# Sparse attention and an eight-expert MoE on one Trainium2 core: second search's first round moved into the opening gather, and several orders changed

## The chip, the cores and the metric

One core of one Trainium2 chip runs the whole kernel. The time is device microseconds of one execution. Engines: PE (TensorE, matrix products), DVE (VectorE), ACT (ScalarE), POOL (GpSimd), and SP, which here only issues DMAs. Each engine works through its own instructions in the order in which they stand in its queue and waits on semaphores for the others.

## The reference

Attention over 8 batches, 8 heads, 576 positions and head size 64, with masks of stride 32 (local for the first four heads, strided for the other four). Its 4608 x 512 output goes to a mixture of eight experts with a capacity of 576 tokens each. Tokens are given to experts greedily, by descending gate logit over all (token, expert) pairs:

```python
logits = x @ w_gate
order = np.argsort(-logits.flatten())
for idx in order:
    tok, e = idx // E, idx % E
    if assigned[tok] >= 0 or counts[e] >= cap:
        continue
    assigned[tok] = e
    counts[e] += 1
for e in range(E):
    h = np.maximum(x[assigned == e] @ w1[e], 0.0)
    out[assigned == e] = h @ w2[e]
```

## The kernel before

The attention runs until about 177 us. Then the gate logits L of all tokens are closed (close_last, logits, summit), and the experts are filled one after the other: a "phase" (`ph`, 0 to 7) is one expert in the order in which they fill up.

To find which expert fills next and at which logit, the kernel searches thresholds. A search has seven rounds (`search`, six for the first one, `search0`): DVE compares the best remaining logits with 17 candidate values (`cm`, L862 in the first round, L865 later), PE counts (nine matmuls of L884), DVE copies the counts (`cp`, L888), PE folds them (four matmuls, L892), and DVE reduces to the next base `pm` (L901, L904) and makes the next candidates (`cand`, L868; `pre`, L875). After the search come the expert's number, its weights' loads and scales, the slots of its tokens (`slots`), the list of tokens that are left (`close`), and the token numbers (`indices`: a prefix matmul at L956, a scan on DVE at L962, `rv` at L998, the "rows" matmuls at L1012 that turn it into rows, and `pick` at L1020).

Rows: POOL gathers five tiles of rows of x from memory (`xr`, L1129), ACT and DVE split them into an upper and a lower fp16 half (`xg`, L1118 and L1119), and SP issues DMA transposes into `xt` (L1120). For the first expert the transposes are done by PE (L1110), with ACT (L1111) and DVE (L1112) taking the halves out of PSUM.

Weights: SP loads w1 and w2 in four pieces of 512 KB each; ACT squares them (`jk`, L1051) for a scale (`ss`, L1057; matmul at L1059; L208 to L213), ACT makes the upper halves (`w1h`, `w2h`, L1069) and DVE the lower halves (`w1l`, `w2l`, L1070). The fp32 buffer of each weight is single, so a load waits until DVE has taken the lower half of the weight before.

Each phase's products, `hidden` (L1226) and the output stage (L1278), are three fp16 products for each fp32 one: w1h by the upper and the lower half of `xt`, w1l by the upper half. A hidden block has 12 such terms over two column halves; `hh` (ACT, L1233) and `hl` (DVE, L1234) take the result out of PSUM, which has three such buffers. Results `y` (L1288) are scattered by POOL (L1289).

While PE works on phase `ph`, the work for the next experts is threaded into it. PE's order is written by hand: a clock counts the nanoseconds of issued matmuls, each chain of side work has a due time (the numbers `yield`ed, the constants T_...), and the due chain is advanced (`advance`). ACT's order is by hand in phase 0 only; the others' queues are scheduled by priority at build time. In the opening (183 to 215 us) the order is by hand too: `first_round` lays the list of close operations, in which the second search's first compare, the scale's matmul and the first transposes are inserted; HEAT gives counts of dummy matmuls (L1151) in that stretch.

## Time and profile before

| | us |
|---|---|
| median of 3 runs | 667.06 (661.7 to 668.71) |
| the profiled execution | 658.78 |
| its span in the profile | 657.0 |
| PE busy | 583.7 (89%) |
| DVE busy | 461.2 (70%) |
| ACT busy | 328.6 (50%) |
| POOL busy | 108.8 (17%) |
| DMA | 103.4 MB, 157 GB/s mean |

Phases begin, by the first hidden product, at 215.0, 276.6, 334.5, 388.1, 442.0, 496.1, 546.9 and 604.6 us; the last ends at about 652. PE is the engine with most work; a wait of PE in this part of the program is time lost, where a wait of another engine costs nothing unless PE meets it. The granted clock (PEclk) tells at which share of full speed the array ran.

### The profile page before, as it was taken

What the parts mean: (1) busy time and instruction counts of PE and PEld (TensorE: products, weight loads), DVE (VectorE), ACT (ScalarE), POOL (GpSimd) and SP (SyncE); (2) the same over time, 40 slices, a digit from 0 to 9 for tenths busy, and PEclk for the clock granted to TensorE, in tenths of its full rate; (3) what the DMA queues carried; (4) which work ended last, traced back from release to release, by engine and by line L of the source; (5) the groups of instructions that cost most, each with busy time, mean ns of one, the idle gap of its engine ahead of it and who ended that gap; (6) DMA issues with size and microseconds to landing.
All of it is one profiled execution on the core that took longest, in us unless ns stands there. A gap on an engine that the chain in (4) does not pass through costs nothing.

```text
span 657.0 us, 19687 instructions
## 1 busy us (share of the span) xinstructions
PE 583.7 (89%) x8220; PEld 370.8 (56%) x8220; DVE 461.2 (70%) x1431; ACT 328.6 (50%) x553; POOL 108.8 (17%) x124
## 2 busy tenths in 40 slices
PE   7888787898847789899989999999989998799996
PEld 4566565666533665475457457547637645555752
DVE  5878787887887897878697786776787755572210
ACT  2555463654303574842953951862564477562211
POOL 2011100111102001400410420330160131302011
PEclk9779999998957899999999999999999999799999
DMA  8778798786506507804833931860780585741001
GB/s 255 213 250 238 229 274 239 238 245 206 150 2 211 142 1 266 208 1 156 247 72 116 256 103 34 287 137 17 273 169 33 186 239 178 207 82 50 7 25 48
DMA packets 78480, 103.40 MB, mean 157 GB/s; under 512 B 41624, under 2 KB 49522, under 8 KB 78391
## 3 DMA queue, kind: packets, MB, share of 16 engines
q1 hardware_dynamic: 70311, 80.59, 41.9%
q0 software_dynamic: 7360, 21.15, 10.5%
q8 instruction: 64, 1.05, 0.7%
q10 hardware_dynamic: 720, 0.39, 0.2%
q14 instruction: 25, 0.20, 0.1%
HBM read 74.58 MB, written 18.87 MB: 142 GB/s over the span
## 4 chain that ended last, share of the span: by engine, by line
PE 23%; issue 14%; DVE 13%; DMA 8%; ACT 5%; POOL 3%; POOLq 0%; SPq 0%; DVEq 0%; ACTq 0%
PE ph L1226 15%; DMA w<-in_w_dram 5%; PE ph L1278 5%; DVE w1l L1070 2%; POOL xr L1129 2%; ACT jk L1051 2%; DMA xr<-x_scr,idx 2%; DVE cm L865 2%; DVE w2l L1070 1%; POOL out_dram L1289 1%; DVE xg L1119 1%; ACT w2h L1069 1%; DVE hl L1234 1%; ACT w1h L1069 1%; ACT hh L1233 1%
## 5 line engine op out<-in xcount | busy, mean ns | idle before, releaser
L1226 PE MATMUL ph<-xt,w1h 128*128 128x288 f16 (+2 forms) x1024 | 176.0, 289 | 4.8 <-DMA xt<-xg 1.8
L1226 PEld LDWEIGHTS <-w1h 128*128 128x128 f16 x1024 | 98.6, 99 | 30.9 <-issue 3.4
L1226 PE MATMUL ph<-xt,w1l 128*128 128x288 f16 (+2 forms) x512 | 112.1, 289 | 0.0
L1051 ACT ACTIVATE jk<-w 128x1024 f16<-128x1024 f32 x64 | 67.3, 1052 | 66.6 <-DMA w<-in_w_dram 66.2
L1278 PE MATMUL ph<-w2h,hh 128*128 128x512 f16 x256 | 97.2, 380 | 0.0
L1278 PE MATMUL ph<-w2h,hl 128*128 128x512 f16 x256 | 97.1, 379 | 0.0
L1278 PE MATMUL ph<-w2l,hh 128*128 128x512 f16 x256 | 97.0, 379 | 0.0
L1233 ACT ACTIVATE hh<-ph 128x576 f16<-128x576 f32 (+2 forms) x72 | 42.7, 593 | 100.3 <-PE ph L1226 100.3
L1234 DVE SCALAR_TENSOR_TENSOR hl<-ph,hh 128x576 f16<-128x576 f32 (+2 forms) x72 | 49.4, 686 | 57.0 <-ACT hh L1233 56.7
L1289 POOL DMA_INDIRECT out_dram<-y,idx x40 | 47.6, 1190 | 222.0 <-ACT y L1288 204.2
L1278 PEld LDWEIGHTS <-hh 128*128 128x128 f16 x512 | 48.3, 98 | 54.7 <-issue 3.7
L1129 POOL DMA_INDIRECT xr<-x_scr,idx x40 | 41.4, 1035 | 160.4 <-DVE idx L1024 125.1
L1226 PEld LDWEIGHTS <-w1l 128*128 128x128 f16 x512 | 49.7, 98 | 14.3 <-issue 1.8
L1070 DVE SCALAR_TENSOR_TENSOR w1l<-w,w_sw,w1h 128x512 f16<-128x512 f32 x64 | 45.9, 742 | 10.1 <-ACT w1h L1069 10.1
L1070 DVE SCALAR_TENSOR_TENSOR w2l<-w,w_sw,w2h 128x512 f16<-128x512 f32 x64 | 45.5, 742 | 8.2 <-ACT w2h L1069 8.2
L1069 ACT ACTIVATE w2h<-w,w_sw 128x512 f16<-128x512 f32 x64 | 41.1, 709 | 10.3 <-DVE w_sw L213 10.2
L1069 ACT ACTIVATE w1h<-w,w_sw 128x512 f16<-128x512 f32 x64 | 42.3, 708 | 2.6 <-DVE w_sw L213 1.5
L1288 ACT ACTIVATE y<-ph,so 128x512 f32<-128x512 f32 x32 | 21.8, 680 | 42.4 <-PE ph L1278 41.1
L1278 PEld LDWEIGHTS <-hl 128*128 128x128 f16 x256 | 25.0, 98 | 29.4 <-issue 2.1
L468 POOL DMA_DIRECT2D x_scr<-xs x23 | 14.9, 655 | 151.8 <-DVE vsum L307 96.3
L393 ACT ACTIVATE pr<-spa 128x576 f32<-128x576 f32 x32 | 20.7, 648 | 29.5 <-PE spa L390 28.1
L1119 DVE TENSOR_TENSOR xg<-xr,xg 128x512 f16<-128x512 f32 (+1 forms) x37 | 25.0, 688 | 12.0 <-ACT xg L1118 11.9
(542 smaller groups left out, 878.5 us busy)
## 6 DMA issues: line engine op xcount, KB each, us to landing
w<-in_w_dram SPq DMA_DIRECT2D x64, 512.0 KB
v_s<-in_ns_dram SPq DMA_DIRECT2D x28, 195.0 KB
kl<-in_kl_dram SPq DMA_DIRECT2D x16, 304.0 KB
ks<-in_ks_dram SPq DMA_DIRECT2D x16, 288.0 KB
qs<-in_qt_dram SPq DMA_DIRECT2D x16, 288.0 KB
ql<-in_qt_dram SPq DMA_DIRECT2D x16, 288.0 KB
x_scr<-xl SPq DMA_DIRECT2D x8, 512.0 KB
v_l<-in_nl_dram SPq DMA_DIRECT2D x16, 162.5 KB
```

The costliest lines, as they stand in the source:

```text
L393: nc.scalar.activation(pr[:, :S].rearrange("k (h n) -> k h n", h=2), u.sp[p][:, :, :HS], AF.Exp, scale=0.125)
L1051: nc.scalar.activation(jk, wf[:, c * n4:(c + 1) * n4].rearrange("p c f -> p (c f)"), AF.Square, scale=1.41422, accum_out=sq[:, c:c + 1])
L1069: nc.scalar.activation(hi[:, c, f], wf[:, c, f], AF.Copy, scale=s_)
L1070: nc.vector.scalar_tensor_tensor(lo[:, c, f], wf[:, c, f], s_, hi[:, c, f], op0=OP.mult, op1=OP.subtract)
L1119: nc.vector.tensor_tensor(xs[:, 1], xv, xs[:, 0], op=OP.subtract)
L1129: nc.gpsimd.indirect_dma_start(out=xr[:n], out_offset=None, in_=x_rows, in_offset=bass.IndirectOffsetOnAxis(ap=idx[:n, t:t + 1], axis=0))
L1226: nc.tensor.matmul(tile_[:, j, :w], wt[:, d, f * 128:(f + 1) * 128], xt[:, d // 2, xx, d % 2, c], start=(k == 0), stop=(k == 3 * DC - 1))
L1233: nc.scalar.activation(hv, src, AF.Relu)
L1234: nc.vector.scalar_tensor_tensor(lv, src, 0.0, hv, op0=OP.max, op1=OP.subtract)
L1278: nc.tensor.matmul(py, a[:, f, ts_], w[:, f], start=(k == 0), stop=(k == len(todo) - 1))
L1288: nc.scalar.activation(y, py, AF.Copy, scale=so[:, t:t + 1])
L1289: st = nc.gpsimd.indirect_dma_start(out=out_rows, out_offset=bass.IndirectOffsetOnAxis(ap=idx[:n, t:t + 1], axis=0), in_=y[:n], in_offset= ...
```

## The change

- close_last: the logits of the batch before the last, and the point operations of their peaks, move ahead of the last turn of the attention.
- pre0: the first `pre` (128 x 18) is made before the index chain. In `search` the separate `cand` operation falls away, since `pre` is now one operation with two operands; it is made after the yield instead of before.
- first_round: the close list has no insertions any more. After it come the take, round 0 of the second search, and round 1's compare; the scale follows (`after()`) behind the count, the heat of 20 and 3 and 1 around it, then the transposes and the rest.
- split order: the first w1 splits (k = 0 and 1) of phase 0 are ordered behind the two operations that take the transposed tiles.
- hidden: the first two blocks of the first column block go term by term (four of w1h by upper, four of w1h by lower, four of w1l by upper) instead of row chunk by row chunk.
- X2: the second search's third round waits 900 instead of 100.
- T_HOT7, T_LAST: the eighth expert's number, weights and indices come later.
- rows_of: at a phase's end the waiting loop advances only the fetch of that phase, and does not move the clock.

Instructions: DVE 1386 to 1357; PE 6166 to 6167 matmuls; ACT, POOL and SP as many as before. The diff, cut:

```diff
-X1 = 100
+X1, X2 = 100, 900
-HEAT = (8, 18, 5)
+HEAT = (8, 20, 3)
+T_HOT6, T_CLOSE6, T_HOT7, T_LAST = 3200, 9000, 9000, 6000
...
+            logits(B - 2, ps_b.tile([128, 512], F32, name="spb"))
+            ahead_ = summit(2, edge, (B - 1) * S // TP)
+            ahead_[0]()
             p2 = ps_b.tile([128, 512], F32, name="spb")
...
-                    cand = rt.tile([128, J1 + 1], F32, name="cand18")
-                    nc.vector.tensor_scalar(cand, pre, pm, None, op0=OP.add)
...
-                n = 1 if rd == R1 - 2 else J1 + 1
-                if not last:
-                    pre = cand[:, 0:1]
-                    if n > 1:
-                        pre = rt.tile([128, n], F32, name="pre1")
-                        nc.vector.tensor_scalar(pre, steps[:, rd + 1, :n], cand[:, 0:1], None, op0=OP.add)
-            yield pace(T_COUNT) + (X1 if len(closed) == 1 else T_FIRST if rd == 0 else 0)
+            yield pace(T_COUNT) + ((X2 if rd == 2 else X1) if len(closed) == 1 else T_FIRST if rd == 0 else 0)
             with urgent():
+                if rd and not last:
+                    n = 1 if rd == R1 - 2 else J1 + 1
+                    base, pre = pre[:, 0:1], rt.tile([128, n], F32, name=f"pre{n}")
+                    nc.vector.tensor_scalar(pre, steps[:, rd + 1, :n], pm, base, op0=OP.add, op1=OP.add)
...
-        yield T_HOT1 if ph == 1 else T_HOT6 if ph == E - 2 else T_HOT
+        yield {1: T_HOT1, E - 2: T_HOT6, E - 1: T_HOT7}.get(ph, T_HOT)
...
+                if ph == 0 and nch == DC and k <= 1:
+                    if k == 1:
+                        behind(a, turned[0])
+                    behind(b, turned[1])
...
+        nc.vector.tensor_scalar(pre0, steps[:, 1, :J1 + 1], cand0[:, 0:1], None, op0=OP.add)
         idx, sx = drain(indices(0, slot))
...
-            todo.insert(SCALE_AT, after)
-            todo.insert(SCALE_AT + 1, lambda: heat(HEAT[2]))
-            todo.insert(TURN_AT, lambda: [f() for f in first[:TURN_E]])
-            todo.insert(TAKE_AT, lambda: parts_.append(take(slot, src[0])))
-            todo.insert(SEARCH_AT, lambda: parts_.append(next(gen)))
             for f in todo:
                 f()
-            parts_[0]()
+            rest_ = take(slot, src[0])
+            next(gen)
+            next(gen)
+            heat(1)
+            after()
+            step = next(gen)
+            heat(HEAT[2])
+            for f in first[:TURN_E]:
+                f()
+            rest_()
...
+            if ph == E - 1:
+                yield T_LAST
             with urgent():
                 ei, code = number(w8)
...
+        terms = [(wt, xx, d) for d in range(DC) for wt, xx in ((w1h, 0), (w1h, 1), (w1l, 0))]
+        if n == 1 and f < 2 and js[0].start == 0:
+            terms = [(wt, xx, d) for wt, xx in ((w1h, 0), (w1h, 1), (w1l, 0)) for d in range(DC)]
...
-                    c = min(chains, key=lambda c: c[0])
-                    clock = max(clock, c[0])
+                    c = rows_of.get(ph) or min(chains, key=lambda c: c[0])
+                    if ph not in rows_of:
+                        clock = max(clock, c[0])
                     advance(c)
```

Three places show what moves. First ACT at the turn from phase 5 to phase 6. `w1h` (of w_8710 or w_8705) and `w2h` (of w_8719 or w_8714) are the seventh expert's, the `jk` of w_9164 or w_9162 the eighth's w1. Before:

```order
L1069 ACTIVATE w1h<-w_8710,w_sw_8716 128x4x128
L1288 ACTIVATE y<-ph,so 128x512
L1051 ACTIVATE jk,sq<-w_9164 128x1024 x2
L1069 ACTIVATE w2h<-w_8719,w_sw_8725 128x512 x4
L1288 ACTIVATE y<-ph,so 128x512
L1069 ACTIVATE w2h<-w_8719,w_sw_8725 128x512 x4
L1051 ACTIVATE jk,sq<-w_9164 128x1024
L1233 ACTIVATE hh<-ph 128x576
```

and of the changed kernel:

```order
L1075 ACTIVATE w1h<-w_8705,w_sw_8711 128x4x128 x2
L1304 ACTIVATE y<-ph,so 128x512
L1075 ACTIVATE w2h<-w_8714,w_sw_8720 128x512 x5
L1251 ACTIVATE hh<-ph 128x576
L1075 ACTIVATE w2h<-w_8714,w_sw_8720 128x512 x3
L1057 ACTIVATE jk,sq<-w_9162 128x1024
L1251 ACTIVATE hh<-ph 128x576
L1057 ACTIVATE jk,sq<-w_9162 128x1024 x2
```

The squares of the eighth expert's w1 stood ahead of the seventh's w2 splits; they now stand behind all of them, between the `hh`.

Second, DVE in the opening. Before, from the end of the close list (L204) to the halves of the transposed tiles (L1112):

```order
L204 TENSOR_TENSOR ohn<-ohn,wmn 128x288
L1057 TENSOR_REDUCE ss<-sq 128x1
L208 TENSOR_SCALAR ss_e<-pr__4339 128x1
L209 TENSOR_SCALAR ss_e<-ss_e 128x1
L210 TENSOR_SCALAR ss_e<-ss_e 128x1
L213 TENSOR_SCALAR w_sw_4187<-ss_e 128x2
L982 TENSOR_SCALAR pen<-slot 128x36
L983 TENSOR_TENSOR rmn<-rmn,pen 128x36
L862 TENSOR_TENSOR cm<-rmn,cand_3841 128x612
L875 TENSOR_SCALAR pre_4356<-steps,cand_3841 128x18
L1070 SCALAR_TENSOR_TENSOR w1l<-w_4181,w_sw_4187,w1h 128x4x128 x2
L1112 TENSOR_TENSOR xt<-ph,xt 128x2x2x128 x2
```

and of the changed kernel, from the second search's first compare (L872) on:

```order
L872 TENSOR_TENSOR cm<-rmn,cand_3841 128x612
L894 CAST cp<-pr__4346 128x68
L1063 TENSOR_REDUCE ss<-sq 128x1
L208 TENSOR_SCALAR ss_e<-pr__4361 128x1
L209 TENSOR_SCALAR ss_e<-ss_e 128x1
L210 TENSOR_SCALAR ss_e<-ss_e 128x1
L213 TENSOR_SCALAR w_sw_4188<-ss_e 128x2
L907 SCALAR_TENSOR_TENSOR g_4372,ne<-pr__4346,steps 128x17
L910 TENSOR_REDUCE pm<-ne 128x1
L875 SCALAR_TENSOR_TENSOR cm<-pre_3842,pm,rmn 128x612
L885 TENSOR_SCALAR pre_4429<-steps,pm,pre_3842 128x18
L1122 TENSOR_TENSOR xt<-ph,xt 128x2x2x128 x2
```

The compare, with the `pen` and `rmn` before it, stands ahead of the scale's sum; the next compare follows behind the scale, and the halves of the transposed tiles stand ahead of the first lower weight halves.

Third, POOL, whose queue carries the gathers (`xr`) and the scatters (`out_dram`); the rows of the changed kernel with the gathers for phases 4, 5 and 6:

```order
L1139 DMA xr<-x_scr,idx 128x512 x2
L1305 DMA out_dram<-y,idx 4608x512
L1139 DMA xr<-x_scr,idx 128x512 x2
L1139 DMA xr<-x_scr,idx 64x512
L1305 DMA out_dram<-y,idx 4608x512 x5
L1139 DMA xr<-x_scr,idx 128x512 x4
L1139 DMA xr<-x_scr,idx 64x512
L1305 DMA out_dram<-y,idx 4608x512 x3
L1139 DMA xr<-x_scr,idx 128x512
L1305 DMA out_dram<-y,idx 4608x512
```

Before, the five gathers of a phase always stood together; here an output row stands between the second and the third gather, and later behind a first one.

## Rows read from the trace of the kernel before

**Rows 1.** The page's part 1: busy us (share) and instructions of each engine.

```profile
PE 583.7 (89%) x8220; PEld 370.8 (56%) x8220; DVE 461.2 (70%) x1431; ACT 328.6 (50%) x553; POOL 108.8 (17%) x124
```

**Rows 2.** Waits of PE, 215 to 652: tile, line, releaser: total, times, longest us.

```profile
PE pr__9288 L1012 <- DVE rv L998: 5.5, 1, 5.5
PE ph L1226 <- DMA xt<-xg: 1.8, 2, 1.2
PE pr__4810 L884 <- DVE cm L862: 1.8, 1, 1.8
PE pr__6086 L884 <- DVE cm L865: 1.4, 1, 1.4
...
PE pr__5872 L1059 <- DVE p L1015: 1.2, 1, 1.2
```

**Rows 3.** Stretches: length, busy PE, PEld, DVE, ACT, POOL, PEclk, DMA share, GB/s.

```profile
215.00:651.90 436.90, 413.09 (x3341) 253.70 (x3340) 292.80 (x878) 232.06 (x396) 83.14 (x74) 0.99 0.45 132
215.00:248.98 33.98, 29.13 (x289) 21.52 (x289) 30.31 (x99) 20.28 (x40) 0.00 (x0) 0.95 0.22 61
276.58:303.08 26.50, 25.31 (x244) 19.40 (x245) 18.84 (x58) 9.59 (x16) 0.97 (x1) 1.00 0.06 15
303.08:334.52 31.44, 27.27 (x216) 12.83 (x214) 24.71 (x82) 21.41 (x37) 10.64 (x10) 1.00 0.84 239
467.07:496.06 28.99, 27.05 (x214) 12.64 (x212) 21.75 (x64) 21.04 (x37) 12.45 (x9) 1.00 0.80 215
546.94:580.87 33.93, 27.62 (x234) 20.67 (x233) 19.68 (x44) 23.34 (x41) 6.06 (x6) 0.90 0.71 198
604.64:628.16 23.52, 23.52 (x194) 18.79 (x193) 5.30 (x7) 5.25 (x8) 0.97 (x1) 1.00 0.03 12
```

**Rows 4.** Order of time, PE, phase 6: start, us, line, operation, [idle before].

```profile
562.33 1.51 PE L1012 MATMUL pr__9288<-ohl,rv 128*32 128x64 f16 x36 [5.47 <-DVE rv L998]
...
563.99 1.17 PE L1226 MATMUL ph<-xt,w1h 128*128 128x288 f16 x4
...
568.35 0.65 PE L1226 MATMUL ph<-xt,w1h 128*128 128x288 f16 x4
```

**Rows 5.** Order of time, ACT, turn of phase 5 to 6.

```profile
548.22 1.06 ACT L1051 ACTIVATE jk<-w 128x1024 f16<-128x1024 f32 x1 [4.35 <-DMA w<-in_w_dram]
...
550.72 2.54 ACT L1069 ACTIVATE w2h<-w,w_sw 128x512 f16<-128x512 f32 x4
```

**Rows 6.** Order of time, DVE, phase 6.

```profile
557.14 0.29 DVE L962 TENSOR_TENSOR_SCAN inc<-ones_f,pr__9220 128x72 f32<-128x72 f32 x1
...
561.62 0.66 DVE L998 TENSOR_TENSOR rv<-ohh,val 128x972 f16<-128x972 f16 x1
```

**Rows 7.** Order of time, POOL's first gather, and PE, start of phase 1.

```profile
261.41 0.98 POOL L1129 DMA_INDIRECT xr<-x_scr,idx  x1 [0.30 <-DVE ss_e L208]
...
278.06 0.54 PE L1226 MATMUL ph<-xt,w1h 128*128 128x288 f16 x3 [1.19 <-DMA xt<-xg]
```

**Rows 8.** Order of time, gather of phase 4's rows: POOL, SP, PE.

```profile
419.88 0.98 POOL L1129 DMA_INDIRECT xr<-x_scr,idx  x1 [29.14 <-DVE idx L1024]
...
425.75 8.80 SPq L1120 DMA_TRANSPOSE xt<-xg  x5
...
441.99 0.65 PE L1226 MATMUL ph<-xt,w1h 128*128 128x288 f16 x4
```

**Rows 9.** Order of time, DVE, opening.

```profile
211.52 0.16 DVE L1057 TENSOR_REDUCE ss<-sq 128x1 bf16<-128x4 f32 x1 [1.77 <-ACT jk L1051]
...
212.98 0.80 DVE L862 TENSOR_TENSOR cm<-rmn,cand 128x612 f16<-128x612 f32 x1
...
215.16 1.28 DVE L1112 TENSOR_TENSOR xt<-ph,xt 128x512 f16<-128x512 f32 x2
```

**Rows 10.** Order of time, PE, end of the first hidden block of phase 0.

```profile
219.17 0.98 PE L1110 MATMUL ph<-ident,xr 128*128 128x128 f32 x4
```

**Rows 11.** One line's instructions: `cand`, durations min/median/max, first and last start.

```profile
L868 DVE TENSOR_SCALAR cand<-pre,pm x30: 221/230/233, 223.6 to 502.8; 128x18 f32<-128x18 f32 x30
```

More of the change, by code (lines that the diff above doesn't have):

```diff
@@ L551, in close_last @@
             nc.vector.tensor_copy(xt[:, 1, b], p2[:, :b.stop - b.start])
+            for f in ahead_[1:-1]:
+                f()
             pb = ps_b.tile([128, 512], F32, name="spb")
@@ L556, in close_last @@
             nc.vector.tensor_scalar(lt[:, b], pb[:, :b.stop - b.start], sc, None, op0=OP.mult)
-            logits(B - 2, ps_b.tile([128, 512], F32, name="spb"))
-            for f in summit(2, edge, (B - 1) * S // TP):
-                f()
+            ahead_[-1]()
             logits(B - 1, po_all[:, 1])
@@ L764, in band_stride_attention_then_capacity_moe @@
     cand0 = r1.tile([128, J1 + 1], F32, name="cand0")
+    pre0 = r1.tile([128, J1 + 1], F32, name="pre0")
     def tables():
@@ L778, in band_stride_attention_then_capacity_moe, with behind @@
     scat, closed, first, second = [], [], [], []
-    ready, emitted, rush = set(), set(), set()
+    ready, emitted, rush, rows_of = set(), set(), set(), {}
+    turned = {}
+    def behind(ins, other):
+        tc.add_manual_dep(ins.ins, other.ins.name, mybir.DependencyInfo(mybir.DependencyClass.NoSync,
+                                                                        mybir.DependencyReason.DATA), reason="order")
     def urgent(ph=1):
@@ L853, in search @@
     def search(rm, ohc, more):
-        cand, src, top, pm = cand0, rm, None, None
+        cand, pre, src, top, pm = cand0, pre0, rm, None, None
         ohv = ohc.rearrange("p c e -> p (c e)")
@@ L1065, in parts, with split @@
                 return [(slice(k, k + 1), slice(0, width)) for k in range(nch)]
-            def split(c, f, k, wf=wf, sc=sc, hi=hi, lo=lo):
+            def split(c, f, k, wf=wf, sc=sc, hi=hi, lo=lo, nch=nch):
                 s_ = sc.bitcast(F32)[:, 0:1]
-                nc.scalar.activation(hi[:, c, f], wf[:, c, f], AF.Copy, scale=s_)
-                nc.vector.scalar_tensor_tensor(lo[:, c, f], wf[:, c, f], s_, hi[:, c, f], op0=OP.mult,
-                                               op1=OP.subtract)
+                a = nc.scalar.activation(hi[:, c, f], wf[:, c, f], AF.Copy, scale=s_)
+                b = nc.vector.scalar_tensor_tensor(lo[:, c, f], wf[:, c, f], s_, hi[:, c, f], op0=OP.mult,
+                                                   op1=OP.subtract)
+                if ph == 0 and nch == DC and k <= 1:
+                    if k == 1:
+                        behind(a, turned[0])
+                    behind(b, turned[1])
             todo.append([(T_SQ, lambda c=c, g=square: g(c)) for c in range(4)])
@@ L1110, in turn @@
                 nc.tensor.transpose(pt[:, c // 2, c % 2, :n], xr[:n, c * 128:c * 128 + 128], ident[:n, :n])
[L1111 to L1112 removed]
+            turned[0] = nc.scalar.activation(xs[:, 0], pt[..., :n], AF.Copy)
+            turned[1] = nc.vector.tensor_tensor(xs[:, 1], pt[..., :n], xs[:, 0], op=OP.subtract)
     def halve(ph, xt, xr, t, n):
@@ L1195, in side @@
             slot = yield from slots(ph, *src, code, mv)
-            chains.append([due_now() + (T_F if 1 < ph < E - 2 else 0), fetch(ph, slot, wts)])
+            rows_of[ph] = [due_now() + (T_F if 1 < ph < E - 2 else 0), fetch(ph, slot, wts)]
+            chains.append(rows_of[ph])
             if ph == E - 2:
@@ L1221, in hidden @@
         n = len(js)
-        for d in range(DC):
-            for wt, xs in ((w1h, (0, 1)), (w1l, (0,))):
-                for xx in xs:
-                    for j, c in enumerate(js):
-                        nc.tensor.matmul(tile_[:, j, :w], wt[:, d, f * 128:(f + 1) * 128],
-                                         xt[:, d // 2, xx, d % 2, c], start=(k == 0), stop=(k == 3 * DC - 1))
-                        yield w * 123 // HC
-                    k += 1
+        terms = [(wt, xx, d) for d in range(DC) for wt, xx in ((w1h, 0), (w1h, 1), (w1l, 0))]
+        if n == 1 and f < 2 and js[0].start == 0:
+            terms = [(wt, xx, d) for wt, xx in ((w1h, 0), (w1h, 1), (w1l, 0)) for d in range(DC)]
+        for wt, xx, d in terms:
+            for j, c in enumerate(js):
+                nc.tensor.matmul(tile_[:, j, :w], wt[:, d, f * 128:(f + 1) * 128], xt[:, d // 2, xx, d % 2, c],
+                                 start=(k == 0), stop=(k == 3 * DC - 1))
+                yield w * 123 // HC
+            k += 1
         hv, lv = (a[:, f, js[0].start:js[-1].stop].rearrange("p (j n) -> p j n", j=n) for a in (hh, hl))
@@ L1238, in ffn @@
         if ph == E - 1:
-            dr = nc.gpsimd.drain()
-            tc.add_manual_dep(dr.ins, scat[-1].ins.name, mybir.DependencyInfo(mybir.DependencyClass.NoSync,
-                                                                             mybir.DependencyReason.DATA), reason="pause")
+            behind(nc.gpsimd.drain(), scat[-1])
         hh = xp.tile([128, FC, CAP], F16, name="hh", bufs=1)
```

9 lines of the change are left out of this document (3 added, 6 removed).

## The prediction

> **What bounds the kernel now.** I read the page first: PE works 89% of the span [rows 1], no other engine comes near it. From the first matmul of the experts (215.0) to the end of the last (651.9) PE is busy 413.1 of 436.9 us [rows 3], so about 24 us are idle there, and that, with what the clock loses, is what a change of order can win. The second view is the list of PE's waits in that stretch [rows 2]. One wait stands out: 5.5 us in front of the "rows" matmuls of L1012. Behind it come two waits on the transposed rows `xt` (1.8 us together), two on compares (`cm`, 1.8 and 1.4 us) and one on `p` (1.2). The third view is the table of stretches [rows 3]: the hidden stage of the seventh expert (phase 6, 546.94 to 580.87) takes 33.93 us at a mean clock of 0.90, while the hidden stage of the eighth, beside which nothing is prepared, takes 23.52 at 1.00. Ten microseconds lie in that one stage. The output stage of phase 1 takes 31.44 us where that of phase 4 takes 28.99.
>
> The cause of the large wait is read off three engines in a row. ACT stands before `jk`, the sum of squares of the eighth expert's w1, until 548.22, because the load of that weight has not landed (4.35 us idle) [rows 5]. Only behind it, at 550.72, can it split the seventh expert's w2, which it could have done earlier. DVE takes the lower halves as ACT delivers them; its scan starts at 557.14 and its `rv`, which L1012 reads, at 561.62 [rows 6]. PE is idle for 5.5 us [rows 4], and its clock then stands at half: four matmuls take 1.17 us at 563.99 and 0.65 us at 568.35 [rows 4].
>
> **The change, part by part.**
>
> *Phase 6 (T_HOT7, T_LAST).* The orders show ACT splitting all of w2 before the first `jk` of the eighth weight, so ACT no longer waits for a load in front of the splits. On PE the prefix matmul L956, 4.2 us of matmul into the phase before, stands at 10.1 after, and the rows matmul L1012 at 19.1 instead of 8.5. The scale of w2 now comes at the end of phase 5, about a microsecond ahead of phase 6; eight ACT splits (four took 2.54 us [rows 5]) and one `hh` end about 6.6 us into the phase, the DVE halves about 7.5. From scan to the end of `rv` was 5.1 us [rows 6], so `rv` should be there at 10.1 + 5.1 = 15.3, ahead of 19.1. The `jk` of the eighth weight now cover each other with `hh`; by 14 us the last w2 square could make an `hh` about 1.5 us late, and the three PSUM buffers absorb that. Cost left over: prefix, rows, pick and two scales, some 40 small matmuls, 1.3 us (36 of them took 1.51 us at half clock [rows 4]). So hidden stage 23.52 + 1.3 = 24.8 [rows 3], a gain of 33.93 - 24.8 = 9.1; I take **-9.0**. The lower bound is that a wait stays and only the clock comes back (PE busy 27.62 less 24.8, -2.8 [rows 3]), the upper is 33.93 - 23.52 = -10.4.
>
> *Clock.* The row says that after a 5.5 us wait the granted clock fell to half. It did not after the waits of 276 to 278: 1.00 in the stretch that starts at 276.58 [rows 3]. The Trainium skill, TensorE: Matmul & The Clock Gate, section "HAM oscillation — how this bites in real kernels", says that a wait for data can put the array back to the slow clock, and that the matmuls behind it then pay again. The trace agrees at 562, and by that rule a new wait at each later boundary would cost more than its own length, which is a rival below.
>
> *Search a round ahead (first_round, X2, pre0).* Round 0 of the second search and the compare of round 1 now run while DVE waited 1.77 us for ACT (209.75 to 211.52 [rows 9]). There are as many rounds in all, but each search runs about 3 us of matmul ahead in phases 0 and 1; the rows matmul of phase 1's successor stands at 29.9 us instead of 32.6, of phase 0's at 28.8 instead of 31.3. The gather that feeds phase 1 was first issued at 261.41 and its last tile let PE go at 278.06, 16.65 us later [rows 7]. The gather comes about 2.5 us of matmul earlier, and one round fewer and less stall lies before it, some 5 us in all, so the 1.8 us of waits on `xt` [rows 2] go: **-1.8**. In phase 1's output the compare that came late (1.4) and the wait on `p` (1.2) [rows 2] stand at places with more room; I let the stage fall from 31.44 to the 28.99 of phase 4 [rows 3], **-2.5**, and take **-0.5** for the round that leaves the phase (13 matmuls). No cover is needed for the removed `cand18`: 30 instructions of 230 ns [rows 11], on an engine that is busy 70%, are worth nothing directly, and I cost them at 0 except in phase 0, where DVE sets the pace (below).
>
> *Opening of the experts.* By hand: `pre0` delays the index chain by 0.15; the close of the list ends at 209.9; the compare (0.80 [rows 9]) fits before 211.3; the sum `ss`, which was at 211.52, comes at 211.7 behind a `cp`, and so do the scale and the first splits, 0.2 late. Against that PE no longer needs the second operand early: the first four terms use only the upper halves, and DVE makes `xt`'s lower half before `w1l`, at 214.3 instead of 215.16 [rows 9]. The first column block should end at 216.7 to 217.7 where it ended at 219.17 [rows 10]: 1.5 to 2.5 us won. But from 215 to 248.98 DVE is busy 30.31 of 33.98 us [rows 3], so most of that is given back to DVE: at the end of the stage the last compare, 1.8 us late before [rows 2], is late by about 2.4. I take **-1.0**, bounds 0 and -3. The logits of close_last move the last reduce by 0.1: **-0.1**, bounds -0.4 and +0.2.
>
> *What is paid.* In phases 2 to 5 the rows of the next expert come later: the rows matmul moves from 26.0 us of matmul to 30.1, 30.6 and 31.1 (phases 2 to 4) and from 22.2 to 27.9 in phase 5, since the count that stood at 43.3, the end of a phase, now stands 0.7 us into the next, and the hidden stage holds four rounds instead of three. What may be late next is `xt` at the next phase's start. In phase 3, whose gather serves phase 4, the first gather was issued at 419.88, the five transposes started at 425.75 and took 8.80 us, and PE began at 441.99 [rows 8]. So 7.4 us lie between the end of those transposes and the start, and 4 to 6 are now used. For the rows fetched in phases 2 to 4 I hold 0 to 2 us of stall possible; in phase 3 POOL, whose DMAs are in order, has an output row between two gathers, which adds 1.3 (a gather took 0.98 with 0.30 idle before it [rows 7]), and phase 5 has the same and a table load of SP between two transposes, 1 us. I take nothing for the start of phase 3, **+1.0** for that of phase 4, **+0.3** for that of phase 5, and **+1.0** for phase 5 and its end (half a microsecond of stall at the start of phase 6, and one round more). The bounds: nothing (7.4 us of room suffice), and +4 each.
>
> Sum: -9.0 - 1.8 - 2.5 - 0.5 - 1.0 - 0.1 + 1.0 + 0.3 + 1.0 = -12.6 us. The profiled execution took 658.78 us (span 657.0), so 646.2, or 1.9% less. The median of the runs, 667.06, is 1.3% above the profiled one, and they lie between 661.7 and 668.7; 667.06 x 0.981 = 654.3, forecast **654 us**.
>
> **The rivals.**
>
> *Rows late at each boundary, slower than before.* The later rows in phases 2 to 5 make `xt` late at the starts of phases 3 to 6. It decides from 12.6 / 4 = 3.2 us each beyond what I charged, where the gain is gone; slower by over 1% from about 4.9 each. For it: the chain from gather to tile is 16.65 in phase 1 [rows 7], and 4.1 to 5.7 us are taken from it four times; and if each wait is as long as the one at 562 [rows 2], the clock falls to half behind it [rows 4]. Against it: the 7.4 us of room [rows 8], and no wait on `xt` stands among PE's there today, only the two of 276 to 278 [rows 2]. Price with 3.2 each: 658.8 on the profiled scale, no change (667); with 5 each: 674.
>
> *The phase-6 wait stands somewhere else.* The eighth weight's squares come in between `hh`s; if a load lands late again, `hh` waits on ACT instead and PE with it. Half the gain stays: -8.1, 650.7, or 659 on the scale of the runs. For it: ACT has now waited there for a load [rows 5]; against it: PE has three buffers.
>
> *The opening does not do what it says.* The first matmul waits for the landing of the rows, or PE runs it at half clock as it did (0.95 mean in the stretch [rows 3]), and DVE, the bound there, gives back all: -11.6, 655.
>
> *More than that.* The boundaries stay free and the opening keeps 2.5: about -16.5, 650.
>
> **How the numbers follow.** My forecast as it stands has 0.43, the opening without gain 0.16, the phase-6 wait elsewhere 0.14, rows late 0.19 (11 of these 19 between -1% and +1%, 8 beyond +1%), more than that 0.08. A measurement of this kernel tells about 1% from no change. Faster by over 1%: 0.43 + 0.16 + 0.08 + half of the phase-6 rival, 0.07 = 0.74. Same: 0.07 + 0.11 = 0.18. Slower: 0.08. The range goes from 645 (more than that, with runs as scattered as those of before) to 665 (rows late by nearly 3 us each); the likeliest case alone has 649 to 660.
>
> **What would show it.** In the changed profile the wait on `rv` in front of the rows matmul is gone, ACT's longest idle time before a `jk` of the eighth weight has no split behind it, and the clock is 1.00 from 546 to the end; the hidden stage of phase 6 takes 24 to 26 us. No wait on `xt` at phase 1's start. At the starts of phases 4 and 6 small waits on `xt`, under 1.5 us. The first column block ends 1.5 us or more earlier, and the hidden stage of phase 0 ends at most 3 us earlier. Wrong is the forecast if PE waits over 3 us at two boundaries, or if the hidden stage of phase 6 still takes over 29 us.

## The result, and the profile after

The changed kernel runs in 657.02 us (median of 20; before, in the same sessions, 666.94, also 20): 0.988 of the time before, with a 95% interval of 0.985 to 0.991. The forecast was 654 us, in the range 645 to 665: faster, by 1.2% where 1.9% was expected. The ratio leaves out the executions that took over 1.5% longer than the fastest of their kernel, so it is not the quotient of the two medians. The profiled execution spans 650.8 us where the one before spanned 657.0.

PE is still the engine that works most, and a little more of the span [rows 1]:

```profile
PE 587.8 (90%) x8221; PEld 371.7 (57%) x8221; DVE 459.0 (71%) x1402; ACT 329.4 (51%) x553; POOL 105.7 (16%) x124
```

The waits of PE among the experts (tile, line, what it waited for: total, times, longest us). The 5.5 us on `rv` of [rows 2] is gone; a wait of 3.6 us on a compare has taken the first place. The two waits on `xt` at the start of phase 1 are gone too, and one of 0.6 us stands at the start of phase 6:

```profile
PE pr__7525 L890 <- DVE cm L875: 3.6, 1, 3.6
PE pr__4778 L890 <- DVE cm L872: 2.4, 1, 2.4
PE pr__9390 L1026 <- DVE p L1021: 1.7, 1, 1.7
PE pr__5983 L890 <- DVE cm L875: 1.6, 1, 1.6
PE pr__8153 L1065 <- DVE p L1021: 1.4, 1, 1.4
...
PE ph L1244 <- DMA xt<-xg: 0.6, 1, 0.6
```

The stretches that answer to [rows 3], now the hidden stage of phase 0, the outputs of phases 1, 3, 4 and 5, and the hidden stages of phases 6 and 7 (length, busy PE, PEld, DVE, ACT, POOL, PEclk, DMA share, GB/s):

```profile
215.52:247.67 32.15, 27.50 (x278) 20.18 (x277) 29.25 (x95) 20.53 (x41) 0.27 (x2) 1.00 0.26 79
...
300.48:329.83 29.35, 27.16 (x201) 12.54 (x199) 21.63 (x63) 19.97 (x34) 11.02 (x9) 1.00 0.91 249
...
408.91:440.43 31.52, 27.93 (x204) 12.97 (x202) 22.67 (x64) 20.09 (x34) 9.47 (x9) 0.95 0.77 237
...
465.56:496.03 30.47, 28.30 (x203) 12.80 (x201) 22.50 (x67) 19.97 (x34) 9.81 (x9) 0.94 0.83 243
...
521.17:546.94 25.77, 25.47 (x165) 11.70 (x162) 15.12 (x56) 17.97 (x32) 8.09 (x8) 1.00 0.90 279
546.94:574.84 27.90, 25.57 (x235) 19.81 (x234) 21.81 (x53) 24.69 (x44) 4.14 (x4) 1.00 0.50 177
...
598.40:621.92 23.52, 23.52 (x193) 18.79 (x192) 5.30 (x7) 5.24 (x8) 0.97 (x1) 1.00 0.04 13
```

Read against before: the hidden stage of phase 0 takes 32.15 instead of 33.98, at a clock of 1.00 instead of 0.95, the output of phase 1 29.35 instead of 31.44, the hidden stage of phase 6 27.90 instead of 33.93, at a clock of 1.00 instead of 0.90. Two stages became longer with a mean clock below 1: the output of phase 3 (31.52, before 28.79) and that of phase 4 (30.47, before 28.99). That of phase 5 became longer as well (25.77, before 23.59), but its hidden stage is shorter by as much (25.14, before 27.29). From first to last expert matmul it is 430.1 us, before 436.9: 6.8 us less. Stage by stage that is 13.7 us of gains and 6.9 of losses, or 11.5 and 4.7 with phase 5 taken as one.

**The new wait in phase 3.** Two views in one fence, in order of time: PE (the fold of one search round and the next round's count), and DVE (the lower halves `xg` of the next expert's rows, `g` and `pm` of the search, and the compare `cm` that PE's count reads):

```profile
426.94 0.25 PE L898 MATMUL pr__7453<-cp,fold 128*128 128x17 f16 x4
...
434.64 0.33 PE L890 MATMUL pr__7525<-cm,ohn 128*32 128x68 f16 x9 [3.55 <-DVE cm L875]
...
428.23 0.69 DVE L1129 TENSOR_TENSOR xg<-xr,xg 128x512 f16<-128x512 f32 x1 [1.16 <-ACT xg L1128]
...
430.38 0.69 DVE L1129 TENSOR_TENSOR xg<-xr,xg 128x512 f16<-128x512 f32 x1 [0.95 <-ACT xg L1128]
430.99 0.17 DVE L907 SCALAR_TENSOR_TENSOR g<-pr__7453,steps 128x17 f32<-128x17 f32 x1
...
432.39 0.68 DVE L1129 TENSOR_TENSOR xg<-xr,xg 64x512 f16<-64x512 f32 x1 [1.22 <-ACT xg L1128]
433.00 0.20 DVE L910 TRANSPOSE_TENSOR_REDUCE pm<-ne 128x1 f32<-128x32 f32 x1
...
433.75 0.84 DVE L875 SCALAR_TENSOR_TENSOR cm<-pre,pm,rmn 128x612 f16<-128x612 f32 x1
```

The fold was done at 427.2. `g`, which reads it, starts at 430.99, because two halves stand ahead of it in DVE's queue and wait 1.16 and 0.95 us for rows that are still on their way; a third half stands ahead of `pm`, and waits 1.22. So `cm` comes at 433.75 and PE stands still for 3.55 us. The granted clock is at half, the lower of its two levels, in the stretch behind it:

```profile
434.60:437.00 2.40, 2.36 (x14) 0.90 (x14) 2.31 (x5) 0.77 (x2) 1.33 (x1) 0.50 0.22 34
```

**Phase 6.** ACT now splits all of w2 first (`w2h`, from 550.21) and begins the eighth weight's squares only at 555.66; the load, for which ACT waited in [rows 5], has landed by then:

```profile
550.21 3.17 ACT L1075 ACTIVATE w2h<-w,w_sw 128x512 f16<-128x512 f32 x5 [0.82 <-DVE w_sw L213]
...
555.66 1.04 ACT L1057 ACTIVATE jk<-w 128x1024 f16<-128x1024 f32 x1
```

What is left there is 1.65 us on the cast `p` (L1021). It stands behind a weight split on DVE that itself waited for ACT:

```profile
570.33 0.75 DVE L1076 SCALAR_TENSOR_TENSOR w1l<-w,w_sw,w1h 128x512 f16<-128x512 f32 x1 [0.79 <-ACT w1h L1075]
571.00 0.22 DVE L1021 CAST p<-pr__9344 128x64 f16<-128x64 f32 x1
```

**The opening.** PE waits 1.2 us at the third block for the first `hh`, which stands behind seven weight splits on ACT:

```profile
215.36 4.39 ACT L1075 ACTIVATE w1h<-w,w_sw 128x512 f16<-128x512 f32 x7
219.64 0.37 ACT L1251 ACTIVATE hh<-ph 128x256 f16<-128x256 f32 x1
```

### The profile page after: what moved, and what is told of

Its sections match the earlier page's. It is cut to its first block, busy times and chain, and to the rows that moved or that the text cites. A ratio compares the mean times of both kernels' runs of the same rounds, so it can differ in the third digit from the quotient of the medians.

```text
span 650.8 us, 19669 instructions
## 1 busy us (share of the span) xinstructions
PE 587.8 (90%) x8221; PEld 371.7 (57%) x8221; DVE 459.0 (71%) x1402; ACT 329.4 (51%) x553; POOL 105.7 (16%) x124
## 4 chain that ended last, share of the span: by engine, by line
PE 38%; DVE 21%; issue 20%; DMA 9%; POOL 5%; ACT 5%; SPq 1%; POOLq 0%; DVEq 0%; ACTq 0%
PE ph L1244 15%; PE ph L1294 4%; DMA xr<-x_scr,idx 3%; PE spa L367 3%; POOL xr L1139 3%; PE po L422 3%; DMA w<-in_w_dram 3%; POOL out_dram L1305 2%; DVE w1l L1076 2%; ACT jk L1057 2%; DVE w2l L1076 1%; DVE v_l L345 1%; DVE hl L1252 1%; PE spb L512 1%; DVE cm L875 1%
## 5 line engine op out<-in xcount | busy, mean ns | idle before, releaser
L1244 PE MATMUL ph<-xt,w1h 128*128 128x288 f16 (+2 forms) x1024 | 174.0, 286 | 2.9 <-ACT hh L1251 1.2
L1244 PEld LDWEIGHTS <-w1h 128*128 128x128 f16 x1024 | 97.2, 98 | 29.1 <-issue 2.0
L1244 PE MATMUL ph<-xt,w1l 128*128 128x288 f16 (+2 forms) x512 | 109.6, 286 | 0.0
L1294 PE MATMUL ph<-w2l,hh 128*128 128x512 f16 x256 | 98.4, 384 | 0.0
L1305 POOL DMA_INDIRECT out_dram<-y,idx x40 | 42.5, 1062 | 285.1 <-ACT y L1304 278.8
L1139 POOL DMA_INDIRECT xr<-x_scr,idx x40 | 43.5, 1087 | 93.1 <-DVE idx L1030 36.4
L1294 PEld LDWEIGHTS <-hl 128*128 128x128 f16 x256 | 25.2, 99 | 28.5 <-issue 1.2
```

The lines of the kernel that those rows point to most:

```text
L1139: nc.gpsimd.indirect_dma_start(out=xr[:n], out_offset=None, in_=x_rows, in_offset=bass.IndirectOffsetOnAxis(ap=idx[:n, t:t + 1], axis=0))
L1244: nc.tensor.matmul(tile_[:, j, :w], wt[:, d, f * 128:(f + 1) * 128], xt[:, d // 2, xx, d % 2, c], start=(k == 0), stop=(k == 3 * DC - 1))
L1294: nc.tensor.matmul(py, a[:, f, ts_], w[:, f], start=(k == 0), stop=(k == len(todo) - 1))
L1305: st = nc.gpsimd.indirect_dma_start(out=out_rows, out_offset=bass.IndirectOffsetOnAxis(ap=idx[:n, t:t + 1], axis=0), in_=y[:n], in_offset= ...
```

## The experiments

Single executions of one kernel differ by 1% and more here, so the stages of the profiles (each one execution) tell where time goes, and the ratios how much. A ratio is the time divided by that of the kernel before in the same session, with its 95% interval. Line numbers shift by a few with each edit. Four questions: which edit freed phase 6; what the new wait in phase 3 is; who pays for what; and whether a better kernel follows.

**e1, the eighth expert's delays undone in the changed kernel.**

```diff
-            if ph == E - 1:
-                yield T_LAST
-        yield {1: T_HOT1, E - 2: T_HOT6, E - 1: T_HOT7}.get(ph, T_HOT)
+        yield {1: T_HOT1, E - 2: T_HOT6}.get(ph, T_HOT)
```

> The changed kernel with only T_HOT7 and T_LAST undone (the eighth expert's number, weights and indices due as before). Theory A (the eighth list is what gains): the hidden stage of phase 6, 33.9 us before and 27.9 after, goes back to 32 to 34 us with a wait of PE on rv of 4 to 6 us and half clock behind it; ratio to the kernel before 0.996 to 0.999. Theory B (the gain lies in the stages before, the eighth list moves only 2 us): phase 6 at 29 to 30, ratio 0.990 to 0.992.

Ratio 0.9994 (0.995 to 1.004): the gain is gone. The wait on `rv` is back, and that in phase 3's output is there too. But the hidden stage of phase 6 is 31.8 us, not 33.9. So 3.9 of the roughly 7.5 us by which the ratio falls back lie there; this profile has 3.3 more in phase 0, with a stretch at half clock and a wait of 2.0 us of another kind (see e3), and the rest is not assigned.

```profile
PE pr__9231 L1018 <- DVE rv L1004: 4.4, 1, 4.4
PE pr__7525 L890 <- DVE cm L875: 3.8, 1, 3.8
```

**e2, only these delays, in the kernel before.**

```diff
+            if ph == E - 1:
+                yield 6000
-        yield T_HOT1 if ph == 1 else T_HOT6 if ph == E - 2 else T_HOT
+        yield {1: T_HOT1, E - 2: T_HOT6, E - 1: 9000}.get(ph, T_HOT)
```

> The kernel before with only the later eighth expert (the two delays of 9000 and 6000). Theory A: the hidden stage of phase 6 falls from 33.9 to 26 to 28 us, all else as before: 6 to 8 us, ratio 0.988 to 0.991, about all that the whole change gives. Theory B: under 3 us, ratio 0.996 or more.

Ratio 0.993 (0.989 to 0.998), and the stage falls to 31.3, not to 26 to 28. The wait on `rv` is gone from it by these delays alone; PE now waits 2.4 us there on `y` and 1.5 on `hl`. ACT's rows (start, us, line, operation) say why: ACT still waits for the eighth weight's load, 4.24 us, ahead of the split of w2. The order of ACT that I read from the changed kernel is not the work of this edit:

```profile
556.21 1.06 ACT L1051 ACTIVATE jk<-w 128x1024 f16<-128x1024 f32 x1 [4.24 <-DMA w<-in_w_dram]
...
559.81 2.54 ACT L1069 ACTIVATE w2h<-w,w_sw 128x512 f16<-128x512 f32 x4
```

**e3, only the waiting loop as before, in the changed kernel.**

```diff
-                    c = rows_of.get(ph) or min(chains, key=lambda c: c[0])
-                    if ph not in rows_of:
-                        clock = max(clock, c[0])
+                    c = min(chains, key=lambda c: c[0])
+                    clock = max(clock, c[0])
```

> The changed kernel with only the waiting loop as before (any chain is advanced at a phase's end and the clock moves on). It moves the rows matmul of phases 2 to 4 from 30.2 to 31.1 us of matmul back to 25.8. Theory A (later rows cost the waits of 3.6 us in phase 3's output and 1.4 in phase 4's, with half clock behind each): these go, the outputs of phases 3 to 5 lose 1 to 3 us each, 4 to 6 us in all; ratio 0.979 to 0.983. Theory B (those waits come from DVE's order and not from the place of the rows): they stay, and waits at the phases' ends come back as before; ratio 0.987 to 0.991.

Ratio 0.991 (0.986 to 0.996): no gain over the changed kernel's 0.988. The rows come 5 us earlier, and the waits do not go away. They stand before the rows matmul (PE waits 1.9 and 1.4 us for `ohl`, the third of which stands on DVE behind an `hl` that waits for ACT) and at a `cp` in phases 2 to 4. With the loop undone ACT's order is the old one again, with two squares ahead of w2's splits and 4.24 us of waiting for the load in front of them, and still there is no wait on `rv` in phase 6, whose hidden stage takes 29.0. Part of the wait at `cp` cannot be read from this kernel's order: DVE stands 2.42 us for something that the trace calls remote.

```profile
364.33 0.76 DVE L1252 SCALAR_TENSOR_TENSOR hl<-ph,hh 128x576 f16<-128x576 f32 x1 [2.30 <-ACT hh L1251]
365.01 0.55 DVE L1010 TENSOR_TENSOR ohl<-sh,iota 128x768 f16<-128x768 f16 x1
...
437.61 0.23 DVE L894 CAST cp<-pr__7426 128x68 f16<-128x68 f32 x1 [2.42 <-remote]
```

**e4, the two edits on the first blocks undone** (term by term, and the splits behind the tiles).

```diff
-        if n == 1 and f < 2 and js[0].start == 0:
-            terms = [(wt, xx, d) for wt, xx in ((w1h, 0), (w1h, 1), (w1l, 0)) for d in range(DC)]
-                if ph == 0 and nch == DC and k <= 1:
-                    if k == 1:
-                        behind(a, turned[0])
-                    behind(b, turned[1])
```

> The changed kernel without the two edits on phase 0's first blocks (term by term, and the splits ordered behind the tiles). Theory A (what the first blocks win is given back at the wait of 1.2 us for hh behind seven weight splits, and to DVE): hidden stage of phase 0 stays at 32 to 32.8 us; ratio as of the whole change, 0.987 to 0.990. Theory B (the first blocks' gain is kept): it is 33.5 to 34.5 us; ratio 0.990 to 0.992.

Ratio 0.986 (0.977 to 0.995), as of the whole change: these edits do not show in the time. The execution that was profiled is the longest of its four and 5 us late before the experts begin, so its stages are not read here, and the stage itself stays open.

**e5, the halves behind the compare.** In the changed kernel, the third to fifth lower half of a phase's rows are ordered on DVE behind the compare of the round under way:

```diff
+            lower = nc.vector.tensor_tensor(xs[:, 1], xv, xs[:, 0], op=OP.subtract)
+            if 1 <= ph and t >= 2:
+                if ph not in held:
+                    held[ph] = last_cm[-1]
+                behind(lower, held[ph])
```

> The changed kernel with one order added on DVE: of the five lower halves xg of the next expert's rows, the third to fifth stand behind the compare cm of the search round that is under way (before, the third and fourth stood ahead of its g, the fifth ahead of its pm). Theory A (the waits of 3.6 us in phase 3's output and of 1.6 and 1.2 in those of phases 1 and 2 are cm held up on DVE behind halves whose rows have not landed): these waits fall under 0.5 us each and no half clock follows; outputs of phases 1 to 4 lose 1.3, 1, 4 and 0 to 1 us; ratio to the kernel before 0.976 to 0.982. Theory B (cm is late for its own reasons, its fold or the count): the waits stay over 1 us; ratio 0.986 to 0.990. Rival with the other sign: the transposes come later and PE waits for xt at the starts of phases 2 to 5, 1 to 2 us each.

The waits on `cm` in phases 1 and 3 go (phase 3's output 28.3, before the edit 31.5), that in phase 2 falls only from 1.2 to 0.9. So theory A has the mechanism, but the ratio is not the one that went with it. The rival with the other sign comes true as well: four waits on `xt`, 4.2 us together, of which 1.6 at the start of phase 4, and new waits of 1.2 to 1.4 on the `cp` that now stands behind the halves.

```profile
PE ph L1252 <- DMA xt<-xg: 4.2, 4, 1.6
...
PE pr__7525 L900 <- DVE cp L896: 1.4, 1, 1.4
```

DVE's queue is not the only one that the late rows hold up. With the halves out of its way `g` starts 2.7 us behind its fold in phase 3 (before the edit 3.8): it now stands behind a sum `ss` that waits 2.30 us for ACT, whose square `jk` stands behind an upper half `xg` that waits for its rows. From `g` to `cm` it is 0.45 us instead of 2.76; that part is what the edit takes away. ACT, then DVE:

```profile
429.31 0.63 ACT L1132 ACTIVATE xg<-xr 128x512 f16<-128x512 f32 x1 [1.54 <-DMA xr<-x_scr,idx]
429.85 1.04 ACT L1059 ACTIVATE jk<-w 128x1024 f16<-128x1024 f32 x1
...
431.01 0.16 DVE L1065 TENSOR_REDUCE ss<-sq 128x1 bf16<-128x4 f32 x1 [2.30 <-ACT jk L1059]
431.09 0.17 DVE L909 SCALAR_TENSOR_TENSOR g<-pr__7453,steps 128x17 f32<-128x17 f32 x1
```

The experts take 431.3 us, as with the changed kernel (430.1 and, in e6, 432.2). Ratio 0.992 (0.987 to 0.997) beside 0.994 for the changed kernel in the same session (e6): nothing gained.

**e6, the changed kernel again.**

> The changed kernel a second time, on the chip of these runs, to tell which waits belong to the order and which to one execution. Both theories: ratio 0.985 to 0.991; the waits of 2.4 us on the last compare of phase 0, 1.2 us on hh behind seven splits, 3.5 to 4.2 us in phase 3's output and 1.7 us on p in phase 6 come again within 0.5 us if they belong to the order; a wait that is gone or doubled belongs to the execution.

Ratio 0.994 (0.987 to 1.001), a weaker result than the 0.988 of 20 runs each, with which it agrees by its interval. The waits in question came again: 2.42 in phase 0, 1.24 on `hh`, 3.82 in phase 3's output. They belong to the order. The one on `p` was 1.03, and 1.36 stood before it on `hl`: phase 6's hidden stage took 27.98. What did not come again is the clock of phase 0: its hidden stage took 33.4 us at a mean of 0.95, in the first profile 32.15 at 1.00, with the same waits.

**e7, three edits:** e5's, the eighth rows matmul due 1.5 us earlier (`T_HOT7` 7500), close_last as before.

```diff
-T_HOT6, T_CLOSE6, T_HOT7, T_LAST = 3200, 9000, 9000, 6000
+T_HOT6, T_CLOSE6, T_HOT7, T_LAST = 3200, 9000, 7500, 6000
```

> The changed kernel with three edits: the halves behind the compare; the eighth expert's rows matmul due 1.5 us earlier (T_HOT7 7500), which puts the cast p ahead of the first w1 split on DVE; close_last in its old order. Theory A: besides what the halves give, the wait of 1.65 us on p in phase 6 goes (hidden stage 25.5 to 26.5 us) and the opening starts 0.4 us earlier; ratio 0.972 to 0.980. Theory B (each of these waits only covers another): hidden stage of phase 6 stays at 27.5 to 29, ratio 0.984 or more.

Ratio 0.990 (0.984 to 0.995), median 653.2. Theory B: phase 6's hidden stage stays at 29.1, with 1.9 us on `hl` and 1.2 on `p`. The order of close_last hardly tells: from the last two matmuls of L390 in the attention to the first count of the opening search it is 10.72 to 10.91 us in the old order (before, e2, e7, e9, e11; 12.33 in e10) and 10.54 to 11.11 in the new (after, e1, e3, e5, e6, e8, e12, four of them 10.54).

**e8, one of seven splits behind the first `hh`.**

```diff
-            if ph not in rush:
-                yield step if ph else min(step, T_BULK0)
+            if ph not in rush or ph == 0:
+                yield step if ph else min(step, 500)
```

> The changed kernel with the w1 splits of phase 0 spread a little: one of the seven splits that stand ahead of the first hh on ACT stands behind it. Theory A (the 1.2 us wait at the third block is hh behind the splits): the wait falls to 0.5 to 0.7 us, by one split of 0.63. Theory B (the wait is for something else, such as a PSUM buffer that DVE holds): it stays at 1.2 us, as hl ends it.

The wait falls from 1.24 to 0.49 us, as theory A had it; what is left of it the trace puts down to `hl` on DVE, as theory B had it. A new wait of 1.56 us follows at 224.30 for a `w1l` that is late by the same edit. Phase 0's hidden stage is 34.3 us, of which DVE works 29.4. This is a single execution without a ratio.

**e9, only the waiting loop, in the kernel before.** The chain of a phase's rows is kept by its phase, and the loop that waits for the rows drives that chain alone:

```diff
-            chains.append([due_now() + (T_F if 1 < ph < E - 2 else 0), fetch(ph, slot, wts)])
+            rows_of[ph] = [due_now() + (T_F if 1 < ph < E - 2 else 0), fetch(ph, slot, wts)]
+            chains.append(rows_of[ph])
-                    c = min(chains, key=lambda c: c[0])
-                    clock = max(clock, c[0])
+                    c = rows_of.get(ph) or min(chains, key=lambda c: c[0])
+                    if ph not in rows_of:
+                        clock = max(clock, c[0])
```

> The kernel before with only the waiting loop changed (a phase's end advances only its own fetch, the clock stays). Its order puts ACT's splits of the seventh w2 ahead of the eighth's squares, which the eighth's later due times alone do not (e2). Theory C (the loop edit and the eighth edit share phase 6: the first frees ACT, the second moves the rows matmul behind the chain on DVE): hidden stage of phase 6 at 30.5 to 32.5 us, with a wait on rv of 3.5 to 5 us and no wait of ACT for a load ahead of a split; ratio to the kernel before 0.994 to 1.002, since the rows matmul of phases 2 to 4 stands at 33.3 to 34.6 and the halves stand before compares. Theory A (the eighth edit alone): 33 to 34 us as before.

Slower: 1.006 (1.002 to 1.010). Seven waits on `xt`, 12.6 us together, at the starts of phases 1 to 6, the longest 3.9 at phase 5: the rival that ended on the other side, in full.

```profile
PE ph L1228 <- DMA xt<-xg: 12.6, 7, 3.9
PE pr__9114 L1060 <- DVE ss L1058: 3.4, 1, 3.4
PE pr__9288 L1013 <- DVE rv L999: 2.3, 1, 2.3
```

And ACT's w2 splits now begin right behind the scale, with no square ahead of them: it is this edit that reorders ACT. Phase 6 alone takes 32.9, with 2.3 us left on `rv`.

**e10, loop and eighth expert together, in the kernel before** (the diffs of e2 and e9).

> The kernel before with the loop edit and the eighth edit, without the rest. Theory C: hidden stage of phase 6 at 27.5 to 28.5 us, as in the whole change (27.9), where the eighth edit alone gave 31.3; phase 3's output holds a wait of 2 to 4 us; ratio 0.986 to 0.993. Theory A: the two give no more than the eighth alone, 31 us. What the rest of the change (search a round ahead, opening) gives is then the difference to 0.988: theory D says 2 to 4 us, from the waits on xt at phase 1 (1.8 to 1.9) and the output of phase 1 (2).

The hidden stage of phase 6 is 28.5, theory C. But the ratio is 1.002 (0.997 to 1.007), not 0.986 to 0.993: the loop's price at the phases' starts takes all of it.

```profile
PE ph L1230 <- DMA xt<-xg: 11.7, 6, 3.5
PE pr__9114 L1060 <- DVE ss L1058: 3.1, 1, 3.1
```

**e11, rows 1.2 and 1.0 us earlier, with e5's order and the old close_last.**

```diff
-T_FIRST, T_COUNT, T_SUM, T_PREFIX, T_NEXT, T_HOT, T_DUP = 1100, 3700, 1800, 3900, 2300, 4200, 550
+T_FIRST, T_COUNT, T_SUM, T_PREFIX, T_NEXT, T_HOT, T_DUP = 1100, 3700, 1800, 3900, 2300, 3000, 550
-T_HOT6, T_CLOSE6, T_HOT7, T_LAST = 3200, 9000, 9000, 6000
+T_HOT6, T_CLOSE6, T_HOT7, T_LAST = 2200, 9000, 9000, 6000
```

> The changed kernel with the halves behind the compare, close_last in its old order, and the rows matmul of phases 1 to 5 due 1.2 us earlier (T_HOT 3000; T_HOT6 2200); with it POOL's five gathers stand together again. If the rows' way from gather to tile is what binds phases 3 to 5 (waits on xt of 1.6, 0.9 and 1.2 us in e5), the waits at the starts of phases 4 to 6 fall to under 0.6 each, and PE waits at most 1.3 us more per phase for ohl ahead of the rows matmul; sum of the experts 427 to 431 us, ratio 0.975 to 0.985. If DVE's chain to ohl binds instead, the waits move there and the sum stays at 430 to 433, ratio 0.986 to 0.992.

Ratio 0.987 (0.980 to 0.994). The profile has 3.9 us of remote waits on DVE and 434.3 us for the experts; the wait at phase 4's start is 1.6 as in e5. It decides neither way.

**e12, X2 undone in the changed kernel.**

```diff
-X1, X2 = 100, 900
+X1, X2 = 100, 100
```

> The changed kernel with X2 back at 100: the second search's third round comes 0.8 us of matmul earlier, and with it everything in phases 0 to 5 (rows matmul of phases 2 to 4 at 29.5, 30.0, 30.2 instead of 30.2, 30.6, 31.1); POOL's five gathers stand together. Theory E (each microsecond by which the rows come earlier pays, as from e10 to the whole change): the wait in phase 3's output falls under 2 us, no wait on xt, phases 2 to 5 take 1 to 3 us less in all; against it the third round's count in phase 0 waits up to 0.8 us more for its compare; ratio 0.982 to 0.988. Theory F (the wait of phase 3's output is DVE's order alone, and phase 0 is bound by DVE): nothing won, phase 0's hidden stage 0.5 to 1 us longer, ratio 0.988 to 0.992.

Ratio 0.981 (0.976 to 0.986), median 651.6: faster than the kernel before; the changed kernel had 0.988 (0.985 to 0.991) and, in e6, 0.994. Phase 3's output is 28.95, phase 4's 28.1, PE does not wait for `xt`, and the wait on the last compare of phase 0 is 1.3 instead of 2.4. Phase 6 gave 3 us of that back (30.85, two waits on `hl`).

```profile
PE ph L1244 <- DVE hl L1252: 3.1, 2, 1.6
...
PE pr__4767 L890 <- DVE cm L872: 1.3, 1, 1.3
...
PE pr__7521 L890 <- DVE cm L875: 1.2, 1, 1.2
```

So X2 probably costs here; the two kernels did not run in one session. Theory E holds for phases 3 and 4; the loss in phase 0 did not come. Two things move with this edit, the place of the rows and POOL's order: the five gathers of phase 3 stand together again, where the changed kernel had an output row of 0.95 us between the second and the third. The run does not separate them.

**Phase 6 by its two edits** (hidden stage, us, one execution each; e3 and e1 have the rest of the change besides):

| | eighth as before | eighth later |
|---|---|---|
| loop as before | 33.93 (before) | 31.34 (e2), 29.01 (e3) |
| loop changed | 32.85 (e9), 31.79 (e1) | 28.53 (e10), 27.90 and 27.98 (the change, twice) |

The mean clock of the stage is 1.00 in e3 and in the change, and 0.86 to 0.95 in the others. With both edits and further ones beside them the stage takes 27.3 to 30.9 us (e5, e7, e8, e11, e12).

## Why the prediction was right, and where its steps were not

The direction was right, and by the step that carried most of the sum: phase 6 gave most of what was won, and its large wait and half clock went. The size was not right: 1.2% where 1.9% was expected, with three terms mis-sized (phase 6, what is paid, phase 1). In the two profiles the clock adds luck in both directions: half clock in phase 0 of the one before, about 1.4 us, and in phase 4 of the one after, about 1.2.

- **Phase 6, -9.0.** The stage fell by 6.0, to 27.9, where 24 to 26 was named as the sign. Wait and half clock went as the step said. The size was 3 us too large: I had not seen that `p` stands on DVE behind a split that waits for ACT (1.65 us of PE's time here, 1.0 to 1.7 in other profiles), nor the 0.6 us for `xt`, and PE's own work came to 25.57 us where the step had 24.8. The gain was put to one edit and is of two. The wait on `rv` goes by T_HOT7 and T_LAST, as the step said (e2, e3). But they do not move ACT's squares behind w2's splits; the loop does (e2 against e9, e10). In the kernel before, the later eighth alone gives 2.6 us, the loop alone 1.1, both together 5.4; beside the rest of the change the later eighth without the loop gives 4.9 (e3).
- **Clock.** No stretch at half clock is left in phase 6. One stands behind the new wait of 3.55 us in phase 3, and one in phase 4 behind 1.45 us of wait. That a wait of 1.2 us left the clock alone at 276 before, and one of 1.45 us at 476 after did not, no run here explains; the last section has a pair of equal waits with different clocks behind them. The Trainium skill, TensorE: Matmul & The Clock Gate, section "HAM oscillation — how this bites in real kernels", describes what followed the 3.55 us: the matmuls behind a wait run at the slow clock.
- **Phase 1, -1.8 and -3.0.** The waits on `xt` at 276 are gone in every kernel with the search a round ahead and there in every one without (1.9 in e2, 1.5 in e9, 1.7 in e10). The shorter one lay at the end of phase 0's output, which became 0.7 shorter; the stage that held the other became 0.6 shorter, since a wait of 0.5 us on a `cp` has come in. The output of phase 1 gave 2.1 of the 3.0.
- **Opening, -1.0.** The hidden stage of phase 0 gave 1.8 in one execution, 0.6 in the other, but most of that is the clock. At a mean of 1.00 the stage takes 32.54 and 32.55 with the old opening (e2, e9) and 32.15 and 32.16 with the new (the change, e7); at 0.95 it takes 33.98 and 33.39 (before, e10) and 33.41 to 33.65 (e1, e3, e5, e6, e11). So the edits give about 0.4, and the term was too large. The first block did end 1.6 us earlier, as forecast, 2.0 us behind its first matmul instead of 4.2; with the old opening at full clock it is 2.6 to 2.8 (e2, e9), so about 0.7 of the 2.2 is the edits'. Ahead of the experts nothing is shown: from the first count of the opening search to the first expert matmul it is 30.82 and 30.81 us in the two profiles of the change, 31.31 before, but 30.78 to 32.50 in the other kernels with the new opening. The edits on the first blocks have no part that the time shows (e4). Not foreseen was the wait of 1.2 us for `hh` behind seven splits; the late last compare was (2.4, as forecast).
- **What is paid, +2.3.** This is the step that failed. I looked for the later rows at the starts of the next phases, with 7.4 us of room [rows 8], and found room enough; indeed `xt` was late there only once, by 0.6, though the first gather came 4.7 to 7.0 us later in phases 2 to 5. But the rows pass through ACT and DVE on their way, and both work in their queue's order: the late rows held up the search, one stage earlier. Price: 2.7 us in phase 3's output and 1.5 in phase 4's, 4.2 where 1.3 stood; phase 5 cost nothing. Of the 1.5, 1.2 are PE's work at half clock, which e6 did not have there (its stage took 30.0, with more waiting). e5 shows both ends of it: with the search let through first on DVE, the wait on the compare goes and `xt` is late by about as much.
- **The rival with the other sign** was right in mechanism and wrong in degree. The loop alone makes the kernel slower (e9), by the very waits that the rival described; what keeps them away in the whole change must be the search a round ahead, which was put down as a gain of phases 0 and 1 only. From e10 to the whole change is 1.002 to 0.988. No run undoes the search alone; the other parts of that difference were undone in e4 (first blocks), e7 and e11 (close_last) and e12 (X2), and the ratio stayed at 0.981 to 0.990.
- **The sum.** -12.6 forecast, -6.8 measured among the experts. Of the difference 3.0 is phase 6, 2.4 what is paid (4.7 in phases 2 to 5 where 2.3 stood) and 1.4 phase 1 with the end of phase 0's output, less 1.0 that the rest gave beyond the forecast, which the clock in phase 0 more than explains.

## What to carry to other kernels

When work is made later, follow its data through every engine that touches it on the way, not only to its last reader: an in-order engine that waits for the late data holds up all that stands behind it, and freeing one such queue can leave the next engine's holding the same work (e5). Test edits alone and in pairs before putting a gain down to one; here two edits free a stage together, one of them is a loss by itself, and what is left of the change pays for it. Compare stages at like clock before putting a microsecond down to an edit. A delay that was put in to relieve one stage (X2) is worth taking out again once the other edits stand.

## What the runs showed of the hardware

In some executions DVE and ACT wait for something that the trace calls remote: 0.2 to 2.6 us at a time, mostly at `cp` on DVE and `y` on ACT, and up to 6.2 us in all on DVE in one execution (e3). PE then waits with them (3.8 us in e3). These waits are in all seven profiles of two sessions (e1 to e4, and e9 to e11) and in none of the other seven (before, after, e5 to e8, e12), whatever the edit. What this is stays open. Stages of profiles from different sessions can differ by it; the ratios compare within a session.

Behind one and the same wait of PE the granted clock differs from one execution to the next. In the first profile of the change 2.41 us on the last compare of phase 0 end at 240.88, and the clock stays at 1.00 (242.5 to 245.5); in e6, the same kernel, 2.42 us end at 240.29, and it is at half behind them (columns as above, PEclk 0.50):

```profile
241.90:244.90 3.00, 3.00 (x13) 1.73 (x12) 1.99 (x10) 1.00 (x4) 0.00 (x0) 0.50 0.00 0
```
